# In the first block of a fused state-space and gated-MLP kernel, the w1 products of the first two whole-bank features go ahead of their w3 products

## The chip, the cores and the metric

The kernel runs on one core of a Trainium2 chip. The metric is the device time of one execution in microseconds (us), as the median of several runs. TensorE is called PE here, ScalarE ACT, VectorE DVE, GpSimd POOL and SyncE SP, as in the profile; PEld is PE's weight loads, which overlap its matmuls.

## What is computed

The input x has 2048 rows of 512. Each row is layer-normed to xn, and two branches on xn are added to x:

```python
def _A_ref(x, Lambda_re, Lambda_im, B_re, B_im, C_re, C_im, log_dt, Dskip):
    ...
    dt = jnp.exp(log_dt)
    Lam_bar = jnp.exp(dt * Lam)
    B_bar = ((Lam_bar - 1.0) / Lam)[:, None] * Bmat
    Bu = jnp.einsum("bld,pd->blp", x + 0j, B_bar)
    for t in range(L):
        h = Lam_bar[None, :] * h + Bu[:, t, :]
    ...
    y = 2.0 * jnp.einsum("blp,dp->bld", hseq, Cmat).real + x * Dskip[None, None, :]

def _B_ref(x, w1, w3, w2):
    gate = jnp.einsum("bsd,df->bsf", x, w1)
    up = jnp.einsum("bsd,df->bsf", x, w3)
    h = _silu(gate) * up
    out = jnp.einsum("bsf,fd->bsd", h, w2)

xn = _layernorm(x, axis=-1)
return x + _A_ref(xn, ...) + _B_ref(xn, B_w1, B_w3, B_w2)
```

The change concerns `gate` and `up`: 2048 rows, 512 inputs, 1792 outputs, in bfloat16.

## The kernel before

The rows are cut into four blocks of 512. For each block there are three kinds of work on PE. `ssm_in` makes B·xn (32 matmuls, tile bu_ps). `glu_up` makes gate and up, transposed, so that 128 of the 1792 outputs lie on the partitions: 14 pieces of 128, called features here, and for each feature one PSUM tile for gate (g_ps, from w1) and one for up (u_ps, from w3), each a group of four matmuls over the 512 inputs. `y_out` multiplies by w2 and by C into a tile y_ps. In `glu_up`, ACT takes silu of g_ps (line 391) and copies u_ps (line 393) to SBUF, and DVE multiplies the two into hgT (line 400), one feature late.

All PSUM tiles come from one pool of eight buffers, a bank each (`ps_tile`, line 70); a new tile is given a bank that its last user has left, and the matmul that first writes it waits for that.

The order of the instructions on each engine is the order of the program (`manual_schedule`, line 68): no scheduler moves them. DVE's other work (layer norm of the coming blocks, tables, the scan) lies in a queue of tasks with written costs; `drain(rate)` at the end of each feature hands out as many as the rate allows, and `for_act` gives ACT one more piece per feature. So the program order within `glu_up` is the order on PE, ACT and DVE.

The first block is special. Its rows arrive in four pieces of 128, and PE starts on them piece by piece. Four features (0 to 3, the list `begun`) are opened ahead of `glu_up`: `ahead` makes their products with rows 0 to 383, in eight banks, and `glu_up(0, 1.3, begun)` adds the last 128 rows (matmuls of 128 columns) and then goes on with features 4 to 13 on whole banks, 512 columns each. For blocks 1 to 3 `glu_up` is called without `begun`, and all 14 features are on whole banks.

The weights come in several transfers on SP's queue, in this order: w1 and w3 for features 0 to 3 in two halves each (line 115), w1 for features 4 to 7 (line 116), then, behind the transposition of the last 128 rows (line 546) and in `load_next`: w3 for features 4 to 7 (line 119), the next block's x (line 120), w1 and then w3 for features 8 to 13 (`load_w13(8, NFT)`, issued at line 95), Dskip, and the transposed loads of B (line 103). A weight load on PE waits for the transfer that brings its columns.

The lines that matter: 375 (every matmul of gate and up), 386 to 389 (the two tiles of a feature and its two groups), 391, 393 and 400.

Of the kernel before, what the change touches and what calls it, by code (L numbers as in the profile page):

```python
# [20 lines left out]
def kernel(  # L21
# [48 lines left out]
    def ps_tile(name):  # L70
        return psum.tile([P, 512], FP32, name=name, tag="ps")
# [10 lines left out]
    w1_sb = const.tile([P, NDT, F], BF16, name="w1_sb")  # L82
# [65 lines left out]
    begun = [(ps_tile("g_ps"), ps_tile("u_ps")) for _ in range(3)]  # L148
# [209 lines left out]
    def drain(us):  # L358
        credit[0] = min(credit[0] + us, us + 1.5)
        while queue and credit[0] > 0:  # L360
            cost, task = queue.popleft()
            credit[0] -= cost
            task()
# [8 lines left out]
    def glu_mm(b, f, w_sb, ps, ts, dts=range(NDT), joins=False):  # L372

        for dt in dts:
            nc.tensor.matmul(out=ps[:, ts], lhsT=w_sb[:, dt, f * P:(f + 1) * P], rhs=xnTs[b][:, dt, ts],  # L375
                             start=(dt == 0 and not joins), stop=(dt == NDT - 1))

    def glu_up(b, rate, begun=()):
        hg[b] = work.tile([P, NFT, TBLK], BF16, name="hgT")
        late = None  # L380
        for f in range(NFT):
            if f < len(begun):
                g_ps, u_ps = begun[f]
                ts = slice(TBLK - P, TBLK)
            else:
                g_ps, u_ps = ps_tile("g_ps"), ps_tile("u_ps")
                ts = slice(0, TBLK)
            glu_mm(b, f, w1_sb, g_ps, ts)
            glu_mm(b, f, w3_sb, u_ps, ts)
            sl16 = work.tile([P, TBLK], BF16, name="sl16", bufs=4)  # L390
            nc.scalar.activation(out=sl16, in_=g_ps, func=ACT.Silu)  # L391
            up16 = work.tile([P, TBLK], BF16, name="up16", bufs=4)
            nc.scalar.activation(out=up16, in_=u_ps, func=ACT.Copy)  # L393
            if for_act:
                for_act.popleft()()
            if late is not None:
                late()

            def late(f=f, sl16=sl16, up16=up16):
                nc.vector.tensor_tensor(out=hg[b][:, f, :], in0=sl16, in1=up16, op=ALU.mult)  # L400

            drain(rate)
        late()
# [161 lines left out]
    push([(1.2, par_out)])  # L565
    push(ln_tasks(2))
    glu_up(0, 1.3, begun)
    assert not for_act
    ssm_in(0, 0.8)
# [3 lines left out]
    push(res_tasks(2))  # L573
    push(res_tasks(3))
    glu_up(1, 1.35)
    y_out(0, 4.0)
    ssm_in(2, 0.85)
    glu_up(2, 1.35)
    y_out(1, 4.0)
    ssm_in(3, 0.85)  # L580
# [33 lines left out]
```

## Time and profile before

| | |
|---|---|
| time, median of 3 runs | 212.37 us |
| the runs | 212.05, 212.37, 212.59 us |
| the profiled execution | 212.46 us, of which its span 210.7 us |
| granted TensorE clock | full, in all 40 slices of the span |
| PE busy | 206.3 us of the span, 1048 matmuls |
| DVE, ACT busy | 173.3 us, 93.2 us |
| DMA traffic | 13.82 MB, most of it in the first 60 us |

The profile tells the span of one execution, from the first instruction to the last; the time of an execution is a little longer. A line of a timeline has the start, the length, the engine, the line of the code, the operation, the tile written and the tiles read, the form and how many such instructions follow each other; in brackets stands the idle time of the engine before it and what ended it. A matmul's length includes its way through the array, which lies over the next matmul, so that a group of four is shown as 1.03 us while groups follow each other every 0.86 us. The chain is followed back from the last instruction, at each step to what released it or to the instruction before it on its engine.

### The profile page before, as it was taken

How to read it: one execution, taken by the hardware profiler on the slowest of the kernel's cores; microseconds unless marked ns; L12 is line 12 of the kernel's file. 1: busy time of each engine (PE TensorE's matmuls, PEld its weight loads, DVE VectorE, ACT ScalarE, POOL GpSimd, SP SyncE). 2: the span in 40 equal slices, each digit the busy share in tenths (PEclk: the TensorE clock that was granted, in tenths of full speed). 3: DMA queues.
4: the chain of work that ended last, by engine and by line, in shares of the span. 5: the costliest groups of instructions: out<-in, count | busy, mean ns of one | idle time of the engine just before them, and what ended most of it. 6: DMA issues, size and time to landing. Idle time of an engine off the chain costs nothing.

```text
span 210.7 us, 2902 instructions
## 1 busy us (share of the span) xinstructions
PE 206.3 (98%) x1048; PEld 97.9 (46%) x1048; DVE 173.3 (82%) x345; ACT 93.2 (44%) x167; POOL 6.6 (3%) x27
## 2 busy tenths in 40 slices
PE   8999999999999999999999999999999999999994
PEld 3774444444444444444444444444444444444453
DVE  4668999999999999999999999999999999121111
ACT  4679966666666200066666600036666620000000
POOL 2100340000000000000000000000000000000000
PEclk9999999999999999999999999999999999999999
DMA  5789796984100000000004100100000000000110
GB/s 166 242 254 311 135 175 152 354 167 109 40 0 0 0 25 25 28 26 0 0 0 67 37 0 25 50 28 0 2 0 0 3 0 25 26 25 25 39 39 25
DMA packets 25558, 13.82 MB, mean 66 GB/s; under 512 B 16456, under 2 KB 25544, under 8 KB 25544
## 3 DMA queue, kind: packets, MB, share of 16 engines
q1 hardware_dynamic: 25248, 13.38, 25.4%
q10 hardware_dynamic: 296, 0.27, 0.5%
q8 instruction: 8, 0.13, 0.3%
q14 instruction: 6, 0.05, 0.1%
HBM read 7.74 MB, written 2.10 MB: 47 GB/s over the span
## 4 chain that ended last, share of the span: by engine, by line
PE 91%; DMA 4%; DVE 1%; ACT 1%; SPq 0%; issue 0%
PE y_ps L491 23%; PE u_ps L375 21%; PE g_ps L375 21%; PE y_ps L496 13%; PE bu_ps L414 13%; DMA w_sb<-in_B_w_dram 2%; DMA x_blk<-in_A_x_dram 2%; SPq L546 0%; DVE xn L195 0%; ACT L81 0%; DVE stats L167 0%; ACT rstd_all L175 0%; ACT rstd_all L174 0%; DVE xnT L261 0%; DVE mv_all L170 0%
## 5 line engine op out<-in xcount | busy, mean ns | idle before, releaser
L375 PEld LDWEIGHTS <-w_sb 128*128 128x128 bf16 x518 | 47.1, 98 | 50.4 <-DMA w_sb<-in_B_w_dram 1.4
L375 PE MATMUL u_ps<-xnT,w_sb 128*128 128x512 bf16 (+2 forms) x256 | 58.6, 352 | 0.4 <-DMA w_sb<-in_B_w_dram 0.4
L375 PE MATMUL g_ps<-xnT,w_sb 128*128 128x512 bf16 (+2 forms) x262 | 58.4, 348 | 0.3 <-DMA w_sb<-in_B_w_dram 0.3
L491 PE MATMUL y_ps<-w_sb,hgT 128*128 128x512 bf16 (+2 forms) x238 | 51.2, 366 | 0.0
L393 ACT ACTIVATE up<-u_ps 128x512 bf16<-128x512 f32 x56 | 34.2, 611 | 14.9 <-PE u_ps L375 14.9
L416 ACT ACTIVATE u<-bu_ps 128x512 bf16<-128x512 f32 x32 | 19.1, 597 | 46.3 <-PE bu_ps L414 46.3
L391 ACT ACTIVATE sl<-g_ps 128x512 bf16<-128x512 f32 x56 | 34.2, 611 | 11.1 <-PE g_ps L375 11.1
L448 DVE TENSOR_TENSOR_SCAN ab<-r_col,h,ab 128x256 bf16<-128x256 f32 x56 | 37.7, 732 | 0.2
L491 PEld LDWEIGHTS <-hgT 128*128 128x128 bf16 x238 | 22.8, 98 | 25.9
L501 DVE TENSOR_TENSOR o<-y_ps,x_blk 128x512 bf16<-128x512 f32 (+2 forms) x17 | 11.1, 653 | 24.3 <-PE y_ps L496 24.3
L496 PE MATMUL y_ps<-ct,h 128*128 128x512 bf16 (+2 forms) x136 | 30.4, 366 | 0.0
L414 PE MATMUL bu_ps<-xnT,bt 128*128 128x512 bf16 x128 | 28.1, 379 | 0.0
L400 DVE TENSOR_TENSOR hgT<-sl,up 128x512 bf16<-128x512 bf16 x56 | 23.0, 413 | 1.8 <-ACT up L393 1.8
L496 PEld LDWEIGHTS <-h 128*128 128x128 bf16 x136 | 13.0, 98 | 14.7
L414 PEld LDWEIGHTS <-bt 128*128 128x128 bf16 x128 | 12.5, 98 | 15.1
L167 DVE BATCH_NORM_STATS2 stats<-x_blk 128x6 f32<-128x512 bf16 x16 | 10.6, 676 | 4.0 <-DMA x_blk<-in_A_x_dram 4.0
L457 DVE TENSOR_TENSOR ab<-ab,tab_s 128x2048 bf16<-128x2048 bf16 x8 | 9.8, 1222 | 0.2
L453 DVE TENSOR_TENSOR ab<-ab,tab_c 128x2048 bf16<-128x2048 bf16 x8 | 9.8, 1221 | 0.1
L433 DVE TENSOR_TENSOR ab<-u,tab_y 128x2048 bf16<-128x2048 bf16 x8 | 9.7, 1218 | 0.0
L430 DVE TENSOR_TENSOR ab<-u,tab_x 128x2048 bf16<-128x2048 bf16 x8 | 9.7, 1218 | 0.0
L204 DVE TENSOR_TENSOR x_blk<-xd,x_blk 128x512 bf16<-128x512 bf16 x16 | 6.9, 430 | 0.5
L195 DVE TENSOR_SCALAR xn<-x_blk,mv_all,rstd_all 128x512 bf16<-128x512 bf16 (+1 forms) x18 | 6.3, 392 | 0.6 <-ACT rstd_all L175 0.5
(76 smaller groups left out, 80.3 us busy)
## 6 DMA issues: line engine op xcount, KB each, us to landing
out_dram<-o SPq DMA_DIRECT2D x15, 128.0 KB, 1.7
w_sb<-in_B_w_dram SPq DMA_DIRECT2D x1, 1792.0 KB
x_blk<-in_A_x_dram SPq DMA_DIRECT2D x3, 512.0 KB, 5.6
w_sb<-in_B_w_dram SPq DMA_DIRECT2D x2, 768.0 KB, 8.4
w_sb<-in_B_w_dram SPq DMA_DIRECT2D x4, 256.0 KB, 4.9
w_sb<-in_B_w_dram SPq DMA_DIRECT2D x2, 512.0 KB, 4.3
x_blk<-in_A_x_dram SPq DMA_DIRECT2D x2, 128.0 KB, 2.2
x_blk<-in_A_x_dram ACTq DMA_DIRECT2D x1, 256.0 KB, 4.6
```

The costliest lines, as they stand in the source:

```text
L167: nc.vector.bn_stats(out=sums[c], in_=x_blk[c // CPB][:, c % CPB, :])
L375: nc.tensor.matmul(out=ps[:, ts], lhsT=w_sb[:, dt, f * P:(f + 1) * P], rhs=xnTs[b][:, dt, ts], start=(dt == 0 and not joins), stop=(dt == ...
L391: nc.scalar.activation(out=sl16, in_=g_ps, func=ACT.Silu)
L393: nc.scalar.activation(out=up16, in_=u_ps, func=ACT.Copy)
L400: nc.vector.tensor_tensor(out=hg[b][:, f, :], in0=sl16, in1=up16, op=ALU.mult)
L414: nc.tensor.matmul(out=u_ps, lhsT=bt[ri][:, dt, pt * P:(pt + 1) * P], rhs=xnTs[b][:, dt, :], start=(dt == 0), stop=(dt == NDT - 1))
L416: nc.scalar.activation(out=u16[:, :, pt, ri, :], in_=u_ps.rearrange("p (s t) -> p s t", s=NSB), func=ACT.Copy)
L448: nc.vector.tensor_tensor_scan(out=a[:, pt, 2 * ri + 1, :], data0=r_b, data1=a[:, pt, 2 * ri, :], initial=init, op0=ALU.mult, op1=ALU.add)
L453: nc.vector.tensor_tensor(out=a[:, :, 0::2, :], in0=a[:, :, 1::2, :], in1=tab_b("c"), op=ALU.mult)
L491: nc.tensor.matmul(out=y_ps[:, ds], lhsT=hg[b][:, f, cl * P:(cl + 1) * P], rhs=w2_sb[:, f, ds], start=(f == 0), stop=False)
L496: nc.tensor.matmul(out=y_ps[:, ds], lhsT=h_tiles[i][:, pt, ri, h_ts], rhs=ct[ri][:, pt, ds], start=False, stop=(pt == NPT - 1 and ri == 1))
L501: nc.vector.tensor_tensor(out=o16[:, ds], in0=y_ps[:, ds], in1=x_blk[b][:, cl, ds], op=ALU.add)
```

## The change

Only `glu_up` is changed. For a feature that was begun, nothing moves. When the first feature that was not begun is reached (`f == len(begun)` with a list that isn't empty: feature 4 of block 0), the w1 products of this feature and of the next are both issued, each into a tile of its own, and only then the tile for up is taken and the w3 products of feature 4 are issued. At feature 5 the gate tile is there already, and only the w3 group is issued. From feature 6 on, and in blocks 1 to 3, the order is as before. On PE the groups of features 4 and 5 go from w1(4), w3(4), w1(5), w3(5) to w1(4), w1(5), w3(4), w3(5); the tiles are taken from the pool in the same new order. ACT, DVE and the queues keep their order.

```diff
     def glu_up(b, rate, begun=()):
         hg[b] = work.tile([P, NFT, TBLK], BF16, name="hgT")
         late = None
+        gates = {}
         for f in range(NFT):
             if f < len(begun):
                 g_ps, u_ps = begun[f]
                 ts = slice(TBLK - P, TBLK)
+                glu_mm(b, f, w1_sb, g_ps, ts)
             else:
-                g_ps, u_ps = ps_tile("g_ps"), ps_tile("u_ps")
                 ts = slice(0, TBLK)
-            glu_mm(b, f, w1_sb, g_ps, ts)
+
+                for f_g in range(f, f + (2 if begun and f == len(begun) else 1)):
+                    if f_g not in gates:
+                        gates[f_g] = ps_tile("g_ps")
+                        glu_mm(b, f_g, w1_sb, gates[f_g], ts)
+                g_ps, u_ps = gates.pop(f), ps_tile("u_ps")
             glu_mm(b, f, w3_sb, u_ps, ts)
             sl16 = work.tile([P, TBLK], BF16, name="sl16", bufs=4)
             nc.scalar.activation(out=sl16, in_=g_ps, func=ACT.Silu)
```

## The prediction

> **What bounds the kernel now.** I read four views, from the whole to the place of the change. First the page: busy times and the chain that ended last.
>
> ```profile
> span 210.7 us, 2902 instructions
> PE 206.3 (98%) x1048; PEld 97.9 (46%) x1048; DVE 173.3 (82%) x345; ACT 93.2 (44%) x167; POOL 6.6 (3%) x27
> ...
> PE 91%; DMA 4%; DVE 1%; ACT 1%; SPq 0%; issue 0%
> ```
>
> TensorE (PE) is the bound nearly everywhere: 206.3 of 210.7 us busy, and 91% of the chain. So a change gains only where PE stands still, or where its order lets something else stand still later. The DMA share of the chain is two pieces, x_blk and w_sb, both before 16 us. Next, the list of waits; these are the rows in which PE or its weight loads waited for a transfer (us in total, times, longest):
>
> ```profile
> PEld L375 <- DMA w_sb<-in_B_w_dram: 1.4, 2, 0.9
> ...
> PE u_ps L375 <- DMA w_sb<-in_B_w_dram: 0.4, 1, 0.4
> ...
> PE g_ps L375 <- DMA w_sb<-in_B_w_dram: 0.3, 1, 0.3
> ```
>
> Two stops. The one of g_ps (0.3 us) is at 6.38 us, ahead of the changed code. The one of u_ps is the place of the change, seen in the timeline of PE (start us, length us, engine, line, operation, tile, count, idle time before it):
>
> ```profile
> 13.77 1.03 PE L375 MATMUL g_ps<-xnT,w_sb 128*128 128x512 bf16 x4
> 15.17 1.04 PE L375 MATMUL u_ps<-xnT,w_sb 128*128 128x512 bf16 x4 [0.38 <-DMA w_sb<-in_B_w_dram]
> 16.05 1.03 PE L375 MATMUL g_ps<-xnT,w_sb 128*128 128x512 bf16 x4
> ...
> 21.23 1.03 PE L375 MATMUL g_ps<-xnT,w_sb 128*128 128x512 bf16 x4
> 22.09 1.03 PE L375 MATMUL u_ps<-xnT,w_sb 128*128 128x512 bf16 x4
> ```
>
> The first four lines of w1 (13.77) are feature 4, the first on a whole bank; 15.17 is w3 of feature 4, 16.05 w1 of feature 5; 21.23 and 22.09 are feature 8. The chain says what ended the stop:
>
> ```profile
> 10.39 4.74 DMA w_sb<-in_B_w_dram
> 15.13 0.05 issue
> 15.17 1.04 PE u_ps L375 x4
> ```
>
> That is line 119, w3's columns of features 4 to 7: issued at 10.39, landed at 15.13.
>
> **What the stop costs.** Its bracket says 0.38 us, but that is not what a group loses. Groups of four start every 0.86 us when nothing is in the way (16.05, 16.91, 17.77), although each is shown 1.03 long, since a matmul's end overlaps the next one's start. Unstopped, w3 of feature 4 would have begun at 13.77 + 0.863 = 14.64. It began at 15.17, and its group took 0.873 to the next start instead of 0.863. The loss is 0.54 + 0.01 = 0.55 us. The Trainium skill, "TensorE: Matmul & The Clock Gate", Part 2, says the same of a stream: the draining of a matmul lies over the filling of the next, and only an isolated one shows it. By the idle figure the sum would start from 0.38, by the cadence, which the trace bears out, from 0.55.
>
> **The change, part by part.** No instruction is added or removed: 1048 matmuls, 167 on ScalarE (ACT), 345 on VectorE (DVE), the same transfers. Four matmuls (w1, feature 5) move ahead of four (w3, feature 4). No DMA is issued between them, and SP's and POOL's queues hold nothing that waits for PE here, so landings stay where they are. The queued tasks are drained at the same points.
>
> 1. *Feature 5's w1 group in the gap.* It begins at 14.64. Its weights came in one transfer with feature 4's (line 116), already used at 13.77: no wait.
>
> 2. *Feature 4's w3 group.* It would begin at 14.64 + 0.86 = 15.50. After a landing at 15.13 the group began at 15.17 and ran 0.01 long, so the landing bounds it at 15.13 + 0.05 = 15.18: cover to spare 0.31. Gain so far 0.55.
>
> 3. *What is late next.* From feature 5's w3 on, every group is 0.55 earlier, and so are its needs. Feature 8 takes the next transfers. For w3's columns of features 8 to 13 (line 95, the second of its two issues in that stretch) the view of that tile in a window that holds this issue alone gives start and landing:
>
> ```profile
> L95 SPq DMA_DIRECT2D w_sb<-in_B_w_dram x1: 507/507/507, 13.1 to 13.1; - x1
> ...
> DMA to landing us min/median/max: 8.4/8.4/8.4
> ```
>
> To two places the trace has 13.13 and 21.58. Before, this group ran at 22.09, covered. Now it would run at 22.09 − 0.55 = 21.54, and the landing bounds it at 21.58 + 0.05 = 21.63. So 0.09 is lost again. The w1 half went out 1.5 us sooner on the same queue; its sixteenth and last semaphore update stands at 19.59, and feature 8's w1 would start at 20.68: clear by 1.0. The next are B's turned weights: last pieces 24.81 and 29.41, needed from 31.0 and 31.9 on; the second block's turned rows land by 34.79, needed at 37.9. All clear.
>
> 4. *Banks.* PSUM has eight, handed on as ACT empties them. Silu and copy of the four begun features end at 13.01, 13.49, 13.98, 14.48 and later. Feature 5's w1 now takes the second (13.49, needed 14.64), feature 4's w3 the third (13.98, needed 15.50), feature 5's w3 the fourth (14.48, needed 16.36). Later groups had at least 2.8 us between emptied and needed and lose 0.55: nothing. The price if a bank is not free is the second rival.
>
> 5. *ACT and DVE.* Feature 4's copy (line 393) now waits for a group that is 0.33 later (15.50 against 15.17, ended near 16.5). ACT was behind anyway and began that copy at 17.23: hidden by 0.7 us of queued silus and sines; without this cover it would cost ACT 0.3 and PE nothing, its banks having slack. ACT works without a pause from 12.41 to 25.5, DVE nearly so to 60. Neither gets faster, so I looked for what PE needs of them later: the tightest is h for the third row chunk's y, written 9.4 us before PE loads it, and hgT, 19 us before. An earlier PE of 0.46 eats none of that.
>
> Sum: −0.55 + 0.09 = −0.46 us on the chain, and PE leads from there to the end, so all of it arrives. The profiled execution took 212.46 us (span 210.7 and 1.76 around it), 0.09 above the median of the runs, 212.37. I take the difference to the median: 212.37 − 0.46 = **211.91 us**. Bounds of the unknown, the landings in other executions: the part given back is 0 if the tail at 21.58 comes 0.1 sooner (211.82) and all 0.55 if it comes 0.46 later (212.37). The landing at 15.13 can at most be worth the whole moved group, 0.86 (211.51).
>
> **The rivals.**
>
> *The stop only moves (B).* If w3's second half lands at 22.04 or later, its group starts no earlier than before: 212.37. For it: fifteen of the sixteen updates of that landing stand at 19.67 to 20.70, the last one 0.88 later, so one straggler decides. Against: it must come 0.46 later than in the trace. The Trainium skill, "DMA: Bandwidth & Descriptors", says that only the full count of sixteen means landed ("Why a DMA increments its semaphore by 16 and not by 1") and that HBM's latency goes from 0.2 us to 2 under load ("Latency and other measured facts"). The straggler agrees with the first; no run here shows the second. By that figure (an estimate) the whole gain could go.
>
> *A bank is not free: slower (C).* The moved group asks for a bank one place early. If it were handed the bank emptied last of the eight, the copy of feature 3 (15.76 + 0.67 = 16.43), it would start near 16.5, and feature 6's w1 three groups later at 19.1 instead of 17.77: 1.3 us lost, 213.7. It decides from a bank emptied after 15.2 (15.2 + 3 × 0.86 = 17.77). Against: feature 4's w1 ran at 13.77, when only the banks of 13.01 and 13.49 were empty, so they are handed out oldest first.
>
> *More than the sum (D).* If in the timed runs w3's first half lands 0.2 or more later against PE than in the profile, and the second does not, the gain goes to 0.66 or more: 211.7. For it: the three runs lie between 212.05 and 212.59, a spread of 0.54, and DMA landings are the loosest thing in a trace where PE ticks at 0.86. Against: both are on one queue, and what delays the first delays the second.
>
> **How the numbers follow.** About 0.3% (0.64 us) is what a measurement of this kernel can tell from no change; the sum, 0.46, is 0.22%. Forecast 0.45, of which I give 0.09 to a median measured beyond 0.64, the rest within; B 0.20, within; D 0.25, all beyond; C 0.08, slower; 0.02 for a slower case unnamed. Faster 0.09 + 0.25 = 0.34, same 0.36 + 0.20 = 0.56, slower 0.10. The range takes in D (down to 211.4, below the whole group's 211.51 by some of the runs' spread) and B with half the spread above (212.37 + 0.23 = 212.6); C is outside.
>
> **What would show it.** Right: w1, w1, w3, w3 at 13.77, 14.6, 15.5, 16.4 with no bracket; feature 6's w1 near 17.2; a bracket or a start 0.1 late at feature 8's w3 near 21.6; the first bu_ps group near 31.1 instead of 31.59. Wrong: a stop in front of the second w1 group that names ACT (C), a stop at feature 8 of 0.4 us and bu_ps at 31.6 (B), or an idle stretch of PE after 60 us that names DVE.

## The result, and the profile after

The changed kernel takes 211.70 us in the median of 22 runs (211.55 to 212.34), the kernel before 212.34 us (212.05 to 212.74, 22 runs). The ratio is 0.9974, with a 95% interval of 0.9967 to 0.9980: a gain of 0.55 us (0.42 to 0.70); the medians differ by 0.64. The gain is real, since 1 lies outside the interval, and by the ratio smaller than 0.3%. In one experiment below, before_late, two of the six executions had a granted clock of 0.992 instead of 1.0 and took 215.38 and 215.48 us, so that its ratio is raised by them and its median without them is 213.61 instead of 213.69.

The profiled execution took 211.57 us. The page, its same lines as before:

```profile
span 209.8 us, 2901 instructions
PE 206.3 (98%) x1048; PEld 98.1 (47%) x1048; DVE 173.1 (83%) x345; ACT 93.1 (44%) x167; POOL 6.4 (3%) x27
...
PE 98%; DVE 0%; issue 0%
```

PE is busy for as long as before, 206.3 us, in a span that is 0.9 us shorter. The chain that ended last now has no transfer in it at all: followed back from the end it stays on PE to the first matmuls, since nothing stopped PE on the way.

The timeline of PE at the place of the change (start, length, operation, count):

```profile
13.43 1.89 PE L375 MATMUL g_ps<-xnT,w_sb 128*128 128x512 bf16 x8
15.16 1.89 PE L375 MATMUL u_ps<-xnT,w_sb 128*128 128x512 bf16 x8
16.89 1.03 PE L375 MATMUL g_ps<-xnT,w_sb 128*128 128x512 bf16 x4
...
20.34 1.03 PE L375 MATMUL g_ps<-xnT,w_sb 128*128 128x512 bf16 x4
21.20 1.03 PE L375 MATMUL u_ps<-xnT,w_sb 128*128 128x512 bf16 x4
...
30.70 3.62 PE L420 MATMUL bu_ps<-xnT,bt 128*128 128x512 bf16 x16
```

Eight matmuls of w1 (features 4 and 5), then eight of w3, and no bracket: from 13.43 to 30.70 are 20 groups in 17.27 us, 0.863 each. Before, the same stretch ended here:

```profile
31.59 13.98 PE L414 MATMUL bu_ps<-xnT,bt 128*128 128x512 bf16 x64
```

The same 20 groups took 31.59 − 13.77 = 17.82 us. So 0.55 us of the profile's difference lies here, and all of it arrives: from the first bu_ps group to the end of the span both take 179.1 us. The other 0.34 lies ahead of the changed code: the first whole-bank group began at 13.43 instead of 13.77 us. Before, PE stopped for 0.31 us at 6.38 for the first load of w1, which landed at 6.33; after, that load landed at 5.88 and the stop is missing. Whether the earlier start belongs to the change is one of the questions below.

### The profile page after: what moved, and what is told of

Read it like the earlier page. It is cut to its first block, busy times and chain, and to the rows that moved or that the text cites. A ratio compares the mean times of both kernels' runs of the same rounds, so it can differ in the third digit from the quotient of the medians.

```text
span 209.8 us, 2901 instructions
## 1 busy us (share of the span) xinstructions
PE 206.3 (98%) x1048; PEld 98.1 (47%) x1048; DVE 173.1 (83%) x345; ACT 93.1 (44%) x167; POOL 6.4 (3%) x27
## 4 chain that ended last, share of the span: by engine, by line
PE 98%; DVE 0%; issue 0%
PE g_ps L375 23%; PE u_ps L375 23%; PE y_ps L497 23%; PE y_ps L502 13%; PE bu_ps L420 13%; PE g_ps L153 2%; PE xt_ps L254 0%; DVE o L507 0%; PE u_ps L254 0%; PE g_ps L254 0%; PE xt_ps L554 0%
```

## The experiments

In these kernels the groups are named as in the prediction. "Cadence" is the 0.863 us from one group's start to the next. Each kernel stands beside the runs of the kernel before on the same chip; rows with the same time for it were measured together. The ratio is worked out from all the runs; it is not that of the two medians beside it.

| kernel | us, median (runs) | kernel before there | ratio, 95% interval |
|---|---|---|---|
| before_again | 212.37 (12) | 212.25 | 1.0005, 0.9993 to 1.0017 |
| after_again | 211.56 (6) | 212.25 | 0.9963, 0.9949 to 0.9977 |
| before_nowait | 211.72 (11) | 212.25 | 0.9972, 0.9962 to 0.9982 |
| after_nowait | 211.67 (11) | 212.25 | 0.9970, 0.9959 to 0.9980 |
| before_late | 213.69 (6) | 212.15 | 1.0099, 1.0066 to 1.0132 |
| after_late | 212.82 (8) | 212.15 | 1.0030, 1.0020 to 1.0040 |
| hoist3_late | 211.99 (11) | 212.15 | 0.9992, 0.9982 to 1.0002 |
| hoist3 | 211.56 (9) | 212.15 | 0.9975, 0.9966 to 0.9984 |
| hoist6 | 213.23 (6) | 212.32 | 1.0049, 1.0031 to 1.0066 |
| before_early | 211.75 (5) | 212.32 | 0.9980, 0.9965 to 0.9995 |
| hoist4 | 211.68 (12) | 212.44 | 0.9965, 0.9941 to 0.9989 |

### Second traces of both kernels: before_again and after_again

No edit.

> The kernel before once more, for a second trace. Theory 1 (the gain is the stop at feature 4 alone): 212.3 us, a stop of 0.3 to 0.55 us in front of w3's group of feature 4, and the first whole-bank group starts anywhere from 13.4 to 13.8 us, as loads happen to land at the start. Theory 2 (part of the gain lies ahead of the changed code, since in the profile after this group began at 13.43 instead of 13.77 us): it starts at 13.77 us again, within 0.1.

> The changed kernel once more, for a second trace. Theory 1: 211.7 us, no stop at feature 4, and a start of the first whole-bank group anywhere from 13.4 to 13.8 us. Theory 2: 13.43 us again, within 0.1. Theory 3 (the stop moves to feature 8 in part of the executions): a stop of 0.1 us or more in front of w3's group of feature 8.

The timeline of PE in before_again:

```profile
13.54 1.03 PE L375 MATMUL g_ps<-xnT,w_sb 128*128 128x512 bf16 x4
14.91 1.04 PE L375 MATMUL u_ps<-xnT,w_sb 128*128 128x512 bf16 x4 [0.34 <-DMA w_sb<-in_B_w_dram]
15.78 1.03 PE L375 MATMUL g_ps<-xnT,w_sb 128*128 128x512 bf16 x4
```

The old order begins at 13.54 this time, so the start wanders by itself (theory 2 falls), and the stop is there again: 15.78 − 13.54 − 2 × 0.863 = 0.51 us. In after_again, the timeline of PE and then the view of line 119 (issue, time to landing):

```profile
13.36 1.89 PE L375 MATMUL g_ps<-xnT,w_sb 128*128 128x512 bf16 x8
15.08 1.89 PE L375 MATMUL u_ps<-xnT,w_sb 128*128 128x512 bf16 x8
```

```profile
L119 SPq DMA_DIRECT2D w_sb<-in_B_w_dram x1: 572/572/572, 9.8 to 9.8; - x1
...
DMA to landing us min/median/max: 5.2/5.2/5.2
```

Here w3's columns landed at 15.01 (9.79 + 5.2, to two places in the trace), 0.07 us ahead of the group's start at 15.08, and with the 0.05 us that the other stops show between landing and start the cover was all but used up. In the old order this group was due at 13.36 + 0.86 = 14.22, so with this landing the stop would have been 0.84 us. What the change is worth therefore differs between executions: 0.3 to 0.8 by these two traces (0.31 with the landing of the first profile after, 14.55 against 14.29). Worked out in the same way for all nine traces of this document that have the load in its place (line 119), of either order, the stop that the old order has or would have is 0.3 to 1.0 us, some 0.55 in the middle. Theory 3 shows in neither trace of the changed kernel. Here are the load and the group of feature 8's w3 in after_again:

```profile
L95 SPq DMA_DIRECT2D w_sb<-in_B_w_dram x1: 507/507/507, 13.1 to 13.1; - x1
...
DMA to landing us min/median/max: 7.5/7.5/7.5
```

```profile
21.13 1.03 PE L375 MATMUL u_ps<-xnT,w_sb 128*128 128x512 bf16 x4
```

To two places the load was issued at 13.06 and landed at 20.58; its group began at 21.13 without a bracket.

### The stop taken away without moving anything: before_nowait and after_nowait

In the old order (and, in after_nowait, for features 4 and 8 in the new one) the w3 group reads columns that landed early:

```diff
-            glu_mm(b, f, w3_sb, u_ps, ts)
+            glu_mm(b, 0 if begun and f in (4,) else f, w3_sb, u_ps, ts)
```

> The old order, with w3's group of feature 4 reading the columns of feature 0, which landed long before; the output of feature 4 is not the reference's. Theory 1: the stop is gone without any reordering, so the time is that of the changed kernel, 211.7 us (ratio to before 0.997 to 0.998). Theory 2: what lies ahead is unchanged, so 0.2 to 0.3 us of the gain is missing: 212.0. Theory 3: equal to the changed kernel, with the same stop at feature 8.

> The new order, with w3's groups of features 4 and 8 reading the columns of feature 0; the outputs of these two features are not the reference's. Theory 1: nothing is left to gain, 211.7 us, within 0.1 of the changed kernel. Theory 3: feature 8 took back 0.1 us or more in the changed kernel, so this is 0.1 to 0.4 us faster than it, 211.3 to 211.6.

Before_nowait, the timeline of PE:

```profile
13.79 1.03 PE L375 MATMUL g_ps<-xnT,w_sb 128*128 128x512 bf16 x4
14.66 1.03 PE L375 MATMUL u_ps<-xnT,w_sb 128*128 128x512 bf16 x4
15.52 1.03 PE L375 MATMUL g_ps<-xnT,w_sb 128*128 128x512 bf16 x4
```

The old order without the stop runs at the cadence and takes 211.72 us, the time of the changed kernel. The profiled execution began its whole-bank groups at 13.79 us, no earlier than that of the kernel before (13.77), and took 211.94 us, 0.52 less. So the gain is the stop, and the early start in the profile after, 0.34 us, was luck (theory 2 falls a second time). After_nowait, which could not stop at feature 8 either, is at 211.67, no faster than after_again beside it (211.56). The intervals leave room for 0.1 or 0.2 us; with the traces, where feature 8 has half a microsecond to spare, theory 3 falls.

### The landing made later: before_late, after_late, hoist3_late

The load of line 119 is issued behind the next block's x:

```diff
-        nc.sync.dma_start(out=w3_sb[:, :, 4 * P:8 * P], in_=w3v[:, :, 4 * P:8 * P])
         nc.sync.dma_start(out=x_blk[1], in_=xv[:, 1, :, :])
+        nc.sync.dma_start(out=w3_sb[:, :, 4 * P:8 * P], in_=w3v[:, :, 4 * P:8 * P])
```

and hoist3_late puts three w1 groups in front: `f + (3 if begun and f == len(begun) else 1)`.

> The old order, with the load of w3's features 4 to 7 issued behind that of the next block's x (both 512 KB), so that it lands some 1.4 us later. Theory 1 (a stop costs landing minus need, and each group of four moved in front covers 0.863 us of it): a stop of about 2.0 us in front of w3's group of feature 4, 213.8 us, 1.4 above the kernel before.

> The new order with the same later load. Theory 1: the stop is 2.0 - 0.86 = 1.1 us, 212.8 us; the distance to the old order with the later load is the whole moved group, 0.86 us, where it was 0.6 to 0.7 with the load in its place. Rival (the order itself brings a constant gain, whatever the landing): the distance stays at 0.6 us.

> The same later load, with the w1 groups of three features (4, 5, 6) in front instead of two. Theory 1: a stop of about 0.3 us is left, 212.0 us, another 0.8 us below the order with two. Rival (banks: a third tile asked for ahead of time meets a bank that ACT has not emptied): a stop at the third w1 group that names ACT, and less than half of the 0.8 us.

The first w3 group in the timelines of PE of before_late, after_late and hoist3_late (the last cut off by its window):

```profile
16.45 1.04 PE L375 MATMUL u_ps<-xnT,w_sb 128*128 128x512 bf16 x4 [1.87 <-DMA w_sb<-in_B_w_dram]
```

```profile
16.43 1.90 PE L375 MATMUL u_ps<-xnT,w_sb 128*128 128x512 bf16 x8 [0.81 <-ACT up L399]
```

```profile
16.12 2.55 PE L375 MATMUL u_ps<-xnT,w_sb 128*128 128x512 bf16 x11
```

The landings were at 16.41, 16.39 and 16.07, so each group begins 0.04 to 0.05 behind its landing. In after_late the bracket names ACT's copy of feature 3, which ended at 16.40, by chance beside the landing: in the profile after, the same group began at 15.16, and that copy ended only at 16.09. The copy in after_late and in after:

```profile
15.73 0.67 ACT L399 ACTIVATE up<-u_ps 128x512 bf16<-128x512 f32 x1
```

```profile
15.42 0.67 ACT L399 ACTIVATE up<-u_ps 128x512 bf16<-128x512 f32 x1
```

Against the cadence, each counted from its own first whole-bank group (13.55, 13.74, 13.39), the stops are 2.05, 0.98 and 0.15 us, and the medians go down by 0.87 and 0.83 us from one to two to three groups in front (0.79 and 0.83 with the median of 213.61). That is, within the spread, the cadence of a group, 0.863, each time. The gain of a moved group is thus the smaller of two times, its cadence and what is left of the wait, and not a constant of the order: the rival of a constant 0.6 us falls. The third tile met no bank that was not empty.

### More groups in front: hoist3, hoist6, hoist4

The same line with 3, 6 and 4, and the loads in their place.

> Three w1 groups in front, the loads in their place. Theory 1: the stop was covered by two already, so at most 0.1 us faster than the changed kernel (executions in which the load lands late), 211.5 to 211.7 us. Rival (banks): 0.3 us or more slower than the changed kernel.

> Six w1 groups (features 4 to 9) in front of w3's group of feature 4, the loads in their place: six banks are asked for before ACT can copy feature 4, which then waits some 2.5 us longer. Theory 1: ACT makes that up between its pieces (about 1.46 us of work per feature against 1.73 on PE) and the banks come back in time, so 211.6 us as with two and three. Rival (banks): PE stops for a bank that ACT has not emptied, named in its waits, and the time is 212.0 us or more.

> Four w1 groups (features 4 to 7, all the columns that line 116 loaded) in front of w3's group of feature 4. What stopped the order with six was the next w1 load, which landed at 18.09 us; feature 7 needs none of it. If that was all, there is no stop and the time is 211.5 to 211.7 us, as with two and three, though ACT waits for feature 4's copy until about 17.9 us. If banks or ACT's lag also counted there, PE stops behind feature 7, and the time is 211.9 us or more.

With three the time is that of the change, within 0.2 us: 211.56, with a ratio of 0.9975 against 0.9974. In its trace the load landed at 15.43, and the first whole-bank group began at 13.63: two groups in front, up to 15.36, would have left 0.1 us of a stop there. With six both theories missed: the time is in the rival's range, but no bank caused it. The timelines of hoist6, PE and then the weight loads:

```profile
13.39 3.62 PE L375 MATMUL g_ps<-xnT,w_sb 128*128 128x512 bf16 x16
18.14 1.90 PE L375 MATMUL g_ps<-xnT,w_sb 128*128 128x512 bf16 x8 [1.13 <-DMA w_sb<-in_B_w_dram]
19.87 5.34 PE L375 MATMUL u_ps<-xnT,w_sb 128*128 128x512 bf16 x24
```

```profile
18.13 1.84 PEld L375 LDWEIGHTS <-w_sb 128*128 128x128 bf16 x10 [1.62 <-DMA w_sb<-in_B_w_dram]
```

The stop is in front of the fifth group, feature 8, whose w1 columns come in the next transfer (features 8 to 13) and landed at 18.09: due at 16.84, begun at 18.14, 1.30 us. I had counted banks and ACT and not what the moved groups themselves wait for. The median is 0.9 us above the kernel before, since a new stop took the place of the old (1.30 − 0.55 = 0.75 by the traces). Hoist4, which ends just ahead of that transfer, settles the rest (PE, then ACT):

```profile
13.49 3.62 PE L375 MATMUL g_ps<-xnT,w_sb 128*128 128x512 bf16 x15
16.95 3.62 PE L375 MATMUL u_ps<-xnT,w_sb 128*128 128x512 bf16 x16
20.40 1.03 PE L375 MATMUL g_ps<-xnT,w_sb 128*128 128x512 bf16 x4
```

```profile
18.07 0.60 ACT L399 ACTIVATE up<-u_ps 128x512 bf16<-128x512 f32 x1 [0.92 <-PE u_ps L375]
```

No stop on PE (one of the sixteen w1 matmuls is missing from the trace; the starts are at the cadence), although ACT sat idle for 0.92 us and made feature 4's copy at 18.07. The time is 211.68 us, that of the change. In hoist6 ACT waited 3.9 us for that copy, and PE met no bank in use after it either.

### The load issued earlier instead: before_early

```diff
     nc.sync.dma_start(out=w1_sb[:, :, 4 * P:8 * P], in_=w1v[:, :, 4 * P:8 * P])
+    nc.sync.dma_start(out=w3_sb[:, :, 4 * P:8 * P], in_=w3v[:, :, 4 * P:8 * P])
 
     def load_next():
-        nc.sync.dma_start(out=w3_sb[:, :, 4 * P:8 * P], in_=w3v[:, :, 4 * P:8 * P])
```

> The old order, with the load of w3's features 4 to 7 issued right behind w1's (line 116), ahead of the transposition of the last 128 rows. Theory 1: the load lands near 12.5 us, the stop at feature 4 is gone, and as far as that goes the time is 211.7 us; but the transposition's packets queue behind 512 KB (about 1.6 us at some 320 GB/s), so the last rows come 1 us or more later and PE stops for them at the first products of 128 columns: 212.0 to 213.0 us, no better than the change. Rival (the transposition is not held up): 211.7 us.

The timeline of PE (the last line cut off by the window):

```profile
11.37 0.39 PE L375 MATMUL u_ps<-xnT,w_sb 128*128 128x128 bf16 x4
11.81 0.38 PE L375 MATMUL g_ps<-xnT,w_sb 128*128 128x128 bf16 x4
...
13.59 1.03 PE L375 MATMUL g_ps<-xnT,w_sb 128*128 128x512 bf16 x4
14.45 0.81 PE L375 MATMUL u_ps<-xnT,w_sb 128*128 128x512 bf16 x3
```

The load landed at 11.32 and the stop at feature 4 is gone. The transposed rows did come later, 3.1 us behind their issue where it was 2.5 in the kernel before (2.9 at most in another trace, the profile after), but PE stopped for them for only some 0.2 us (11.81 − 11.37, less the 0.22 that a group of four with 128 columns takes). I had that at 1 us or more: the size was wrong, the direction right. At 211.75 us the old order with the earlier load is about as good as the change, by another way.

No version's ratio beats the changed kernel's by more than its interval; hoist3 and hoist4 are level with it.

## Why the prediction was right

The forecast was 211.91 us, a gain of 0.46; measured are 211.70 and, by the ratio, a gain of 0.55 (0.42 to 0.70). The prediction took 0.64 us for the least that can be told from no change; over 22 executions of each kernel the interval is far narrower, and the smaller gain is clear.

*What the stop costs.* The cadence gave 0.55 us where the bracket said 0.38. Taking the stop away by borrowed columns brought the kernel from 212.25 to 211.72, 0.53 us, and the cadence accounts for the steps of 0.87 and 0.83 us in the late kernels, with stops up to 2.05 us. The reading by cadence was right, and the idle figure is short by the end of a matmul that lies over the next start (1.87 in the bracket of before_late, 2.05 against the cadence).

*Feature 5's w1 in the gap, feature 4's w3 covered.* As predicted: w1, w1, w3, w3 with no bracket, and the bu_ps groups 0.55 us earlier measured from the first whole-bank group. The cover to spare, worked out as 0.31, was 0.56 in the profile after (15.16 against 14.55 + 0.05) and 0.02 in after_again: it holds there, and by hoist3's trace it does not hold in every execution.

*The 0.09 us given back at feature 8.* This is the term that was mis-sized: it is nothing. The two traces of the changed kernel have that landing at 20.41 and 20.58 and its need at 21.20 and 21.13, 0.5 us or more to spare. The closest is before_nowait, whose groups follow without a stop too: landing at 21.36, need at 21.56. The profile of before, which I used, had it 8.44 us behind its issue, the longest of all traces here; in the other twelve it is 7.4 to 8.1. The sum rested on one trace where several were needed. Without the term the sum is 0.55 and the time 211.82, the bound that the prediction named for a tail that comes sooner, which the measured gain meets.

*Banks, ACT, DVE.* Costed at nothing, and found at nothing: hoist4 shows PE running on while ACT copies feature 4 a whole microsecond later than in the change.

*The rivals.* B (the stop only moves) did not happen in any trace of the new order with two, three or four groups in front; hoist6 shows it in another form. C (banks, 213.7) did not happen even with four and six tiles asked for ahead. D (0.66 or more) holds for single executions, as after_again shows with 0.84; for the median 0.55 in the middle of the nine traces speaks against it, though the interval, up to 0.70, leaves it room. The argument against D, that what delays the first half delays the second, did not bear out: counted from the first whole-bank group, w3's first half landed 0.3 us later in after_again than in the profile of before, and its second half 0.6 us earlier.

## What to carry to other kernels

When PE waits for a weight load, a group whose weights have landed and whose bank is free can go in front; it covers its own cadence of the wait and no more, and what it moves up must itself have landed. Size a stop on a pipelined engine by the starts of the groups around it, not by the idle time in the bracket. Read several traces before a landing's place, or an early start, is put down to a change or put into a sum: here the start of the first whole-bank group wandered by 0.4 us with no change ahead of it.

## What the runs showed of the hardware

The last of the sixteen updates that make up a landing comes late by very different amounts. For the same 512 KB load (line 119), counted from its issue by the trace's own semaphore updates, the fifteenth and the sixteenth came after 4.54 and 4.74 us in the profile of before, 4.01 and 5.06 in before_again, 3.93 and 5.23 in after_again. Fifteen of the sixteen updates had come up to 1.3 us ahead of the last, and it is behind the last that the groups that waited began, by 0.04 to 0.05 us. What holds the last one back was not tried.
